# Score pairs on the same 128 rows: the key's low part in a zero-padded 128-row buffer

## The chip, the cores and the metric

The kernel runs on one core of one Trainium2 chip. The metric is the device time of one execution in microseconds (us); a time stands for a kernel as the median of its runs.

## What is computed

Causal attention with a decay between positions, then a mixture of experts with one expert per token, all in float32:

```python
B, H, S, D = 2, 8, 576, 64           # attention; 1152 tokens of 512 features
scores = (q @ k.T) / sqrt(D)         # per batch and head
cum = cumsum(log(clip(f, 1e-4, 1)))
scores = where(causal, -1e9, scores + cum[:, None] - cum[None, :])
attn = exp(scores - max(scores)); attn /= attn.sum(-1) + 1e-9
x = concat_heads(attn @ v)           # (1152, 512)
e = argmax(x @ w_gate); gate = softmax(x @ w_gate)[e]
# 8 experts, 288 slots each, first come first served; 512 -> 1024 -> 512
out[i] = gate[i] * (relu(x[i] @ w1[e]) @ w2[e])     # 0 for a token without a slot
```

## The kernel before

The work has two parts. Attention comes first: 16 heads (batch x head), two heads to a group, 8 groups. The experts follow, one after the other, with a code variant for each range of token counts.

A head's queries are cut into five tiles of 128 rows (the last has 64), the loop index `i` of `scores`. Tile `i` meets the keys up to its own end, so its score is 128, 256, 384, 512 or 576 columns wide; 576 is done as 512 and 64. Scores are computed with the fast float format `fp32r`, which rounds its operands, so queries and keys are split in a high and a low part. The tile `hi` holds, for each head, queries in its first S columns and keys in the next S. Its partitions 0 to 63 are the (rounded) values; partitions 64 to 127 hold the queries' low part and, for the keys, the same keys once more. One matmul over 128 rows (L268) thus gives the high and the low part of the query times the key. A second one (L269) adds the query's high part times the key's low part, `kl`, and uses partitions 0 to 63 alone. Both write the same PSUM bank, one of three that take turns (`spsum`).

The buffers belong to a group: `alloc` (L212 on) takes `hi`, `kl`, `raw`, `cd`, `cm` from a pool with two or three turns; `load_main` issues their loads, two on GpSimd's queue (L223, L224) and one on SyncE's (L225). `prep` makes the low parts by subtraction: `kl` at L241, the queries' at L245, mostly on GpSimd, some on VectorE; L243 makes `cm`, decay plus causal mask.

After `scores`, a tile goes through `maxima` (VectorE, L282: adds the decay and takes the row maximum), `exps` (ScalarE, L294), `transposes` (TensorE, L312, through the identity `idf`) and `evac` (copies out of PSUM, ScalarE L325 or VectorE L327). When a half of a group is complete, `av` multiplies by the values (L339, 64 columns of the array per head), `x_out` (L355) brings the result to token order and adds the gate's logits, and `x_evac` divides by the row sums. `route` (L410 to L525, on TensorE from L427) makes the tables of the experts, for the first batch half way through attention.

All engines take their instructions in the order in which the program lists them. That order is found at build time by a list scheduler in the kernel, from hand-set priorities (`BIAS`), assumed costs (S for scores, M for maxima, P for prep, and so on) and dependences; the costs do not know how many rows a matmul uses. `prologue` stands ahead of it, with 12 warm-up matmuls (L143); `filler` matmuls (L399) follow at the start.

In the experts, L847 is the first layer, L862 and L864 or L882 the second (fp32r, 128 rows throughout), L776 and L777 split the weights, L819 transposes the gathered tokens, L907 scatters the results.

Of the kernel before, what the change touches and what calls it, by code (L numbers as in the profile page):

```python
# [7 lines left out]
F32 = mybir.dt.float32  # L8
F32R = mybir.dt.float32r
# [4 lines left out]
ALU = mybir.AluOpType  # L14
# [4 lines left out]
B, H, S, D = 2, 8, 576, 64  # L19
# [5 lines left out]
P = 128  # L25
# [61 lines left out]
def attention_moe(ctx: ExitStack, tc: tile.TileContext, cap, kin, rawin, vin, f, c_iw, w1, w2,  # L87
                  c_mask, c_sel, c_idf, c_tri, c_one, c_pri, c_id, c_iota, c_slot, c_arms, out, dbg=None):
    nc = tc.nc
# [19 lines left out]
    grp = att.enter_context(tc.tile_pool(name="grp", bufs=2))  # L109
    xp = att.enter_context(tc.tile_pool(name="xp", bufs=1))  # L110
# [4 lines left out]
    def spsum(name):  # L115
        turn[0] += 1
        return banks[turn[0] % 3]
# [22 lines left out]
    def prologue():  # L140
        w = spsum("warm")
        for i in range(NWARM):
            nc.tensor.matmul(w, junk[:, :P], junk, start=True, stop=True)  # L143
        fl = pp.tile([BH, S], F32, tag="p", name="fl")
        ones = pp.tile([BH, S], F32, tag="ot", name="ones", bufs=2)
        nc.sync.dma_start(fl, f)
        nc.sync.dma_start(sel, c_sel)
        nc.sync.dma_start(mask[:, :P], c_mask)
        alloc(0)
        load_main(0, 0, 1)  # L150
        load_main(0, 1, 2)
        nc.sync.dma_start(idf, c_idf)
        load_v(0)
        nc.vector.memset(ones, 1.0)
        nc.vector.memset(rsum, 1.0)
        for t in (x_ps, t_ps[0][:, 256:], t_ps[1][:, 256:]):
            nc.vector.memset(t, 0.0)
        nc.vector.tensor_scalar(fl, fl, 1e-4, 1.0, op0=ALU.max, op1=ALU.min)
        nc.scalar.activation(fl, fl, AF.Ln)
        warm = sm.tile([P, 1], F32, tag="nb", name="warm")  # L160
        nc.scalar.activation(warm, rsum[:, 0, 0, 0:1], AF.Exp)
        nc.vector.tensor_tensor_scan(cum, ones, fl, 0.0, op0=ALU.mult, op1=ALU.subtract)
        decay_mm(0)
        for i in range(NWARM2):
            nc.tensor.matmul(w, junk[:, :P], junk, start=True, stop=True)
        nc.vector.tensor_copy(mask[:, P:2 * P], mask[:, :P])
        nc.vector.tensor_copy(mask[:, 2 * P:4 * P], mask[:, :2 * P])
        nc.vector.tensor_copy(mask[:, 4 * P:], mask[:, :S - 4 * P])
        prep(0, 0, nc.vector, 0, 256)
        prep(0, 1, nc.gpsimd, 0, 256)  # L170

    def decay_dst(a, z):
# [4 lines left out]
    def decay_mm(a):  # L177
        for z in range(3):
            t, c0, c1 = decay_dst(a, z)
            nc.tensor.matmul(t, sel[:, a], cum[:, c0:c1], start=True, stop=True)  # L180
# [27 lines left out]

    QA, KA = 0, S
    groups, vt = {}, {}  # L210

    def alloc(g):  # L212
        hi = grp.tile([P, 2, 2 * S], F32R, tag="hi", name=f"hi{g}", bufs=3)
        kl = grp.tile([D, 2, S], F32R, tag="kl", name=f"kl{g}")
        raw = grp.tile([D, 2, 2 * S], F32, tag="raw", name=f"raw{g}")
        cd = grp.tile([P, 2, S], F32, tag="cd", name=f"cd{g}", bufs=3)
        cm = grp.tile([P, 2, S], F32, tag="cm", name=f"cm{g}")
        groups[g] = (hi, kl, raw, cd, cm)

    def load_main(g, z0=0, z1=2):  # L220
        hi, kl, raw = groups[g][:3]
        hs = slice(2 * g + z0, 2 * g + z1)
        nc.gpsimd.dma_start(hi[:, z0:z1, KA:], kin[:, hs])  # L223
        nc.gpsimd.dma_start(hi[:D, z0:z1, :KA], rawin[:, hs, S:])  # L224
        nc.sync.dma_start(raw[:, z0:z1], rawin[:, hs])  # L225
# [4 lines left out]
    def load_group(g):  # L230
        alloc(g)
        load_main(g)

    def load_v(g):
        vt[g] = grp.tile([P, 2, NT, D], F32, tag="v", name=f"v{g}")
        nc.sync.dma_start(vt[g], vin[:, 2 * g:2 * g + 2])

    def prep(h, z, eng, a=0, b=S):
        hi, kl, raw, cd, cm = (x[:, h % 2] for x in groups[h // 2])
        if z == 0:  # L240
            eng.tensor_tensor(kl[:, a:b], raw[:, a:b], hi[:D, KA + a:KA + b].bitcast(F32), op=ALU.subtract)  # L241
        elif z == 2:
            eng.tensor_tensor(cm, cd, mask, op=ALU.add)  # L243
        else:
            eng.tensor_tensor(hi[D:, QA + a:QA + b], raw[:, S + a:S + b], hi[:D, QA + a:QA + b].bitcast(F32),  # L245
                              op=ALU.subtract)
# [9 lines left out]
    def scores(n):  # L256
        h, i = divmod(n, NT)
        j = h % 2
        hi, kl = groups[h // 2][:2]
        r = ROWS[i]  # L260
        q0 = i * P
        w = min(512, q0 + r)
        parts = [(0, w)] if q0 < 512 else [(0, w), (512, r)]
        st[n, "s"] = []
        qa = hi[:, j, QA + q0:QA + q0 + r]
        for c0, cw in parts:
            s = spsum(f"s{n}{c0}") if c0 == 0 else oa_ps[:, SA + D * (h % 2):]
            nc.tensor.matmul(s[:r, :cw], qa, hi[:, j, KA + c0:KA + c0 + cw], start=True, stop=False)  # L268
            nc.tensor.matmul(s[:r, :cw], qa[:D], kl[:, j, c0:c0 + cw], start=False, stop=True)  # L269
            st[n, "s"].append((s, c0, cw))  # L270

    def maxima(n):
# [326 lines left out]
    ctx.enter_context(tc.manual_schedule(engines=MAN))  # L599
    if True:  # L600
        prologue()
        ops, rel = {}, {}

# [13 lines left out]
        for g in range(NPR):  # L617
            tiles = LAST if g == NPR - 1 else TILES
            base = 2 * NT * g
            for z, u in enumerate(tiles):  # L620
                n = 2 * NT * g + u
                h, i = divmod(n, NT)
                half = 0 if i < 2 else 1
                w, r = i * P + ROWS[i], ROWS[i]
                we = (i + 1) * r

                def pr(kind):
                    return base + z + BIAS[kind][0]

                def last(k, d):  # L630
                    return [(k, *prev[-d])] if len(prev) >= d else []

                add("S", h, i, pr("S"), [(pe, 2 * max(107, min(w, 512) / 2.4) + (110 if i == 4 else 0))],
                    lambda n=n: scores(n), [("P", h, z) for z in range(3)] * (n > 1) + [("B", 0, 0)] + last("M", 3) + last("S", 1))
                add("M", h, i, pr("M"), [(dve, t_dve(w) + (77 if i else 0))], lambda n=n: maxima(n),
                    [("S", h, i), ("J", g, 0)] + last("T", 4) + last("M", 1) + [("B", h, q) for q in range(2 if i > 1 else 1)])
                add("E", h, i, pr("E"), [(act, t_act(w) + 93)], lambda n=n: exps(n), [("M", h, i), ("R", g - 2, 0)] + last("E", 1))
                add("T", h, i, pr("T"), [(pe, we / 1.2)], lambda n=n: transposes(n),
                    [("E", h, i)] + last("H", 2) + last("T", 1))
                e = HE[z]  # L640
                add("H", h, i, pr("H"), [(act, t_act(we)) if e == "a" else (dve, t_dve(we))], lambda n=n, e=e: evac(n, e),
                    [("T", h, i)] + [("A", g - 1, q) for q in range(5) if (q > 0) == half])
                prev.append((h, i))
# [22 lines left out]
            for a in range(2):  # L666
                h = 2 * g + a
                if h > 0:
                    for z in range(3 if h > 1 else 2):
                        onv = z == 1 and QE[h % 2] == "d"  # L670
                        add("P", h, z, base + BIAS["P"][3 * a + z], [(dve, t_dve(S)) if onv else (pool, 1360)],
                            lambda h=h, z=z, v=onv: prep(h, z, nc.vector if v else nc.gpsimd),
                            [("I", h // 2, 0)] + [("J", h // 2, 0)] * (z == 2) + [(k, h - 4, i) for k in "SM" for i in range(NT)])
# [51 lines left out]
        while ready:  # L725
            cand = [(max(r, free[ops[n][1][0][0]]), ops[n][0], n, ops[n][1][0][0]) for n, r in ready.items()]
            t, _, _, e0 = min(cand)
# [311 lines left out]
```

## Time and profile before

| | |
|---|---|
| runs | 381.0, 381.79, 383.2 us; median 381.79 |
| profiled execution | span 374.9 us from its first to its last instruction; its own total is not listed beside it |
| TensorE busy | matmul 311.3 us (83%), weight loads 242.0 us (65%) |
| VectorE, ScalarE, GpSimd busy | 182.3 us (49%), 153.5 us (41%), 118.5 us (32%) |
| chain that ended last | PE 60%, issue 17%, DMA 14%, DVE 4% |
| granted TensorE clock, mean | 0.915 |

In the profile PE is TensorE's matmul part, PEld its weight loads, DVE is VectorE, ACT is ScalarE, POOL is GpSimd, SP is SyncE; L12 is line 12 of the kernel. A form such as 64*128 64x512 is rows x columns of the array that a matmul uses, and then its streamed operand, partitions x columns. Busy shares are averages over two parts with different limits, so the first 150 us (attention) and the rest are to be read apart. The chain of waits goes back from the last instruction, at each step to what released it; a row's time is what the step adds to the end, which for pipelined matmuls is less than their own duration. A matmul of plain float32 stands in the trace as two records (L339, L355, L847).

### The profile page before, as it was taken

What the parts mean: (1) busy time and instruction counts of PE and PEld (TensorE: products, weight loads), DVE (VectorE), ACT (ScalarE), POOL (GpSimd) and SP (SyncE); (2) the same over time, 40 slices, a digit from 0 to 9 for tenths busy, and PEclk for the clock granted to TensorE, in tenths of its full rate; (3) what the DMA queues carried; (4) which work ended last, traced back from release to release, by engine and by line L of the source; (5) the groups of instructions that cost most, each with busy time, mean ns of one, the idle gap of its engine ahead of it and who ended that gap; (6) DMA issues with size and microseconds to landing.
All of it is one profiled execution on the core that took longest, in us unless ns stands there. A gap on an engine that the chain in (4) does not pass through costs nothing.

```text
span 374.9 us, 6090 instructions
## 1 busy us (share of the span) xinstructions
PE 311.3 (83%) x1952; PEld 242.0 (65%) x1953; DVE 182.3 (49%) x605; ACT 153.5 (41%) x416; POOL 118.5 (32%) x142
## 2 busy tenths in 40 slices
PE   7999999999999999998659558758658397877980
PEld 3555666566565656988459558757557396877980
DVE  6565667579884654673116107208053251722520
ACT  4364666666663655352044116106241433513510
POOL 4458456673547100254022203203231220300301
PEclk8599999999996999999989969969969879996997
DMA  8993996799271941438992760583917600000001
GB/s 166 252 225 101 251 370 177 138 294 366 62 200 32 388 185 31 146 93 298 410 353 99 270 237 35 203 299 116 405 43 288 243 4 11 30 8 7 34 5 47
DMA packets 19747, 64.86 MB, mean 173 GB/s; under 512 B 3503, under 2 KB 7231, under 8 KB 15074
## 3 DMA queue, kind: packets, MB, share of 16 engines
q1 hardware_dynamic: 12354, 44.86, 36.5%
q0 software_dynamic: 6224, 15.21, 14.8%
q10 hardware_dynamic: 1040, 3.44, 2.5%
q8 instruction: 36, 0.59, 0.7%
q14 instruction: 93, 0.76, 0.6%
HBM read 56.38 MB, written 9.10 MB: 175 GB/s over the span
## 4 chain that ended last, share of the span: by engine, by line
PE 60%; issue 17%; DMA 14%; DVE 4%; ACT 1%; ACTq 1%; DVEq 1%; POOL 0%; SPq 0%; POOLq 0%
DMA out<-yss,six 12%; PE bank L847 11%; PE bank L312 9%; PE bank L269 8%; PE bank L339 7%; PE bank L268 6%; PE bank L882 4%; PE bank L355 3%; PE bank L862 3%; PE bank L577 2%; PE bank L781 1%; DMA wr<-in_w 1%; DMA raw<-in_rawin 1%; PE bank L399 1%; PE bank L819 1%
## 5 line engine op out<-in xcount | busy, mean ns | idle before, releaser
L847 PE MATMUL bank<-xs,wr 128*128 128x128 f32 (+3 forms) x512 | 81.4, 326 | 49.3 <-issue 20.5
L847 PEld LDWEIGHTS bank<-xs,wr 128*128 128x128 f32 x512 | 78.4, 222 | 53.3 <-issue 32.2
L777 DVE TENSOR_TENSOR w2s<-wr,w2s 128x512 fp32r<-128x512 f32 x56 | 44.7, 816 | 74.7 <-ACT w2s L776 54.5
L776 ACT ACTIVATE w2s<-wr 128x512 fp32r<-128x512 f32 x64 | 38.9, 628 | 71.7 <-PE bank L847 40.6
L294 ACT ACTIVATE p<-p,nb 128x128 f32<-128x128 f32 (+4 forms) x80 | 47.6, 597 | 9.6 <-DVE nb L282 9.5
L907 POOL DMA_INDIRECT out<-yss,six x16 | 16.0, 1002 | 108.8 <-ACT yss L899 101.3
L325 ACT ACTIVATE p<-bank 128x256 f32<-128x256 f32 (+4 forms) x56 | 24.8, 448 | 37.3 <-PE bank L312 36.8
L282 DVE CUSTOM_DVE_ANT_0 p<-bank,cd 128x128 f32<-128x128 f32 (+2 forms) x64 | 31.1, 486 | 18.4 <-PE bank L269 10.5
L312 PE MATMUL bank<-idf,p 128*128 128x128 f32 (+2 forms) x240 | 39.2, 276 | 0.4 <-ACT p L294 0.4
L268 PE MATMUL bank<-hi 128*128 128x128 f32 (+5 forms) x96 | 38.1, 397 | 1.6 <-POOL hi L245 1.6
L269 PE MATMUL bank<-kl,hi 64*128 64x128 f32 (+5 forms) x96 | 38.0, 396 | 0.0
L862 PE MATMUL bank<-hs,w2s 128*128 128x304 f32 (+2 forms) x128 | 34.5, 352 | 0.0
L852 ACT ACTIVATE hs<-bank 128x128 fp32r<-128x128 f32 (+3 forms) x64 | 18.5, 293 | 34.6 <-PE bank L847 30.6
L807 POOL DMA_INDIRECT xg<-x_dram,gix x16 | 15.6, 977 | 53.6 <-PE bank L819 19.2
L312 PEld LDWEIGHTS bank<-idf,p 128*128 128x128 f32 (+2 forms) x240 | 23.2, 139 | 14.3 <-issue 5.9
L864 PE MATMUL bank<-hs,w2s 128*128 128x152 f32 (+2 forms) x128 | 30.6, 239 | 0.0
L339 PE MATMUL bank<-p,v 128*64 128x320 f32 (+4 forms) x224 | 30.4, 390 | 0.0
L241 POOL TENSOR_TENSOR kl<-raw,hi 64x576 fp32r<-64x576 f32 x15 | 21.5, 1437 | 15.0 <-PE bank L269 6.4
L269 PEld LDWEIGHTS bank<-kl,hi 64*128 64x128 f32 (+1 forms) x96 | 16.2, 169 | 15.5 <-issue 11.6
L853 DVE SCALAR_TENSOR_TENSOR hs<-bank,hs 128x128 fp32r<-128x128 f32 (+3 forms) x64 | 19.0, 304 | 15.0 <-ACT hs L852 14.8
L882 PE MATMUL bank<-w2s,hs 128*128 128x512 f32 x96 | 25.2, 405 | 0.0
L268 PEld LDWEIGHTS bank<-hi 128*128 128x128 f32 (+1 forms) x96 | 17.4, 181 | 11.4 <-issue 3.9
(142 smaller groups left out, 414.4 us busy)
## 6 DMA issues: line engine op xcount, KB each, us to landing
wr<-in_w SPq DMA_DIRECT2D x27, 1024.0 KB, 12.7
raw<-in_rawin SPq DMA_DIRECT2D x7, 576.0 KB, 8.1
hi<-in_kin POOLq DMA_DIRECT2D x7, 576.0 KB, 12.4
cd<-c_dram SPq DMA_DIRECT2D x7, 576.0 KB, 9.5
wr<-in_w ACTq DMA_DIRECT2D x3, 1024.0 KB, 10.9
v<-in_vin SPq DMA_DIRECT2D x8, 320.0 KB, 4.3
out<-zero SPq DMA_DIRECT2D x8, 288.0 KB, 5.4
wr<-in_w POOLq DMA_DIRECT2D x2, 1024.0 KB
```

What stands on the lines that cost most here:

```text
L268: nc.tensor.matmul(s[:r, :cw], qa, hi[:, j, KA + c0:KA + c0 + cw], start=True, stop=False)
L269: nc.tensor.matmul(s[:r, :cw], qa[:D], kl[:, j, c0:c0 + cw], start=False, stop=True)
L282: nc.vector.tensor_tensor_reduce(p[:r, a:b], s[:r, a - c0:b - c0], src[:r, a:b], -0.125, 1e30 if a == 0 else nb[:r, 0:1], ALU.add, ALU.min ...
L294: nc.scalar.activation(p[:r, :w], p[:r, :w], AF.Exp, bias=bias, scale=-1.0, accum_out=rsum[:r, h // 2 % 2, i, h % 2:h % 2 + 1])
L312: nc.tensor.transpose(t[:kw, c * r:(c + 1) * r], p[:r, c * P:c * P + kw], idf[:r, :r])
L339: nc.tensor.matmul(o[a * D:a * D + D, c0:w], vt[g][:kw, a, c], ps[a][:kw, c, c0:w], start=(c == 0), stop=(c == nk - 1), skip_group_check=True)
L776: nc.scalar.activation(w2s[:, 0, k], raw, AF.Copy)
L777: eng.tensor_tensor(w2s[:, 1, k], raw, w2s[:, 0, k].bitcast(F32), op=ALU.subtract)
L847: nc.tensor.matmul(a[:, :n], w[:, (k % 2) * FF + f * P:(k % 2) * FF + (f + 1) * P], xs[e % 2][k // 2][:, k % 2, :n], start=(k == 0), stop= ...
L862: nc.tensor.matmul(av, w2s[:, 0, k, ds], hs[:, k, :, :n], start=(k == 0), stop=(k == FC - 1), skip_group_check=True)
L864: nc.tensor.matmul(av[:, 0], w2s[:, 1, k, ds], hs[:, k, 0, :n], start=False, stop=(k == FC - 1), skip_group_check=True)
L882: nc.tensor.matmul(y_ps[0][:n], hs[:, k, y, :n], w2s[:, z, k], start=(k == 0 and z + y == 0), stop=(k == FC - 1 and z == 1))
```

## The change

`kl` becomes a buffer of 128 partitions. Its upper 64 partitions (64 to 127) are set to zero once, in the prologue, and never written again; the low part of the keys goes to partitions 0 to 63 as before. L269 (L272 in the changed kernel) then uses all 128 rows of the query tile, so that the query's low part meets zeros and the sum is the same. Both matmuls of a pair now have the same stationary operand and the same form.

For the zeros to stay, the two buffers are no longer taken from the pool by each group but made once (`kls`) and used in turn.

```diff
@@ prologue
         nc.sync.dma_start(idf, c_idf)
         load_v(0)
+        for t in kls:
+            nc.gpsimd.memset(t[D:].bitcast(F32), 0.0)
         nc.vector.memset(ones, 1.0)
...
+    kls = [xp.tile([P, 2, S], F32R, name=f"kl{z}") for z in range(2)]

     def alloc(g):
         hi = grp.tile([P, 2, 2 * S], F32R, tag="hi", name=f"hi{g}", bufs=3)
-        kl = grp.tile([D, 2, S], F32R, tag="kl", name=f"kl{g}")
+        kl = kls[g % 2]
...
@@ prep
-            eng.tensor_tensor(kl[:, a:b], raw[:, a:b], hi[:D, KA + a:KA + b].bitcast(F32), op=ALU.subtract)
+            eng.tensor_tensor(kl[:D, a:b], raw[:, a:b], hi[:D, KA + a:KA + b].bitcast(F32), op=ALU.subtract)
...
@@ scores
             nc.tensor.matmul(s[:r, :cw], qa, hi[:, j, KA + c0:KA + c0 + cw], start=True, stop=False)
-            nc.tensor.matmul(s[:r, :cw], qa[:D], kl[:, j, c0:c0 + cw], start=False, stop=True)
+            nc.tensor.matmul(s[:r, :cw], qa, kl[:, j, c0:c0 + cw], start=False, stop=True)
```

The order on TensorE, VectorE, ScalarE and SyncE stays the same, instruction by instruction. On GpSimd two memsets come in, in the prologue, behind the issues of the first loads (L223, L224; L226, L227 in the changed kernel) and ahead of the first subtraction. Before:

```order
L223 DMA hi_152<-in_kin 128x576
L224 DMA hi_152<-in_rawin 64x576
L245 ISA
L245 TENSOR_TENSOR hi_152<-raw_154,hi_152 64x256
L245 TENSOR_TENSOR hi_152<-raw_154,hi_152 64x320
```

With the change:

```order
L226 DMA hi_154<-in_kin 128x576
L227 DMA hi_154<-in_rawin 64x576
L155 MEMSET kl_114 64x1152
L155 MEMSET kl_115 64x1152
L248 ISA
L248 TENSOR_TENSOR hi_154<-raw_155,hi_154 64x256
L248 TENSOR_TENSOR hi_154<-raw_155,hi_154 64x320
```

The two memsets are new; the rest of GpSimd's list keeps its order. Waits differ on GpSimd alone: with pool buffers the first subtraction into a `kl` (of a group's first head) waited for the last L269 that read either head of the buffer's former group; now it waits for the last L269 of the head whose half it overwrites. The load of the next `hi` (L223), which stood behind that wait, now carries one of its own for the same L269.

## Rows read from the trace of the kernel before

**Rows 1.** The page's 40 equal slices of the span (9.4 us each): busy tenths of TensorE's matmuls and tenths of the granted TensorE clock.

```profile
PE   7999999999999999998659558758658397877980
...
PEclk8599999999996999999989969969969879996997
```

**Rows 2.** Busy time by stretch: the stretch and its length in us, busy us (and instructions) of each engine, granted clock, DMA share and GB/s.

```profile
core 0: us, PE busy (x) PEld busy (x) DVE busy (x) ACT busy (x) POOL busy (x), PEclk, DMA share, GB/s
...
18.00:112.50 94.50, 93.44 (x578) 56.58 (x578) 68.51 (x285) 58.12 (x171) 54.10 (x64) 1.00 0.81 219
86.00:98.30 12.30, 11.70 (x68) 7.35 (x68) 11.37 (x45) 8.32 (x24) 3.20 (x5) 1.00 0.71 230
113.30:120.10 6.80, 6.80 (x27) 3.30 (x25) 3.81 (x14) 2.23 (x6) 4.79 (x5) 0.50 0.14 39
```

**Rows 3.** TensorE's waits between 18 and 145 us, all of them: us in total, times, longest.

```profile
PE bank L427 <- DVE oh L421: 0.6, 1, 0.6
PE bank L312 <- ACT p L294: 0.4, 1, 0.4
```

**Rows 4.** The chain of waits in order of time, 61.3 to 79.1 us: start in us, what the step adds in us, engine, tile and line, and how many instructions in a row.

```profile
62.14 0.42 PE bank L268
62.56 0.43 PE bank L269
62.99 0.48 PE bank L312 x3
...
64.72 0.31 PE bank L269
65.03 0.26 PE bank L268
65.29 0.25 PE bank L269
...
68.68 0.23 PE bank L268
68.91 0.37 PE bank L269
69.27 0.17 PE bank L268
69.45 0.17 PE bank L269
69.62 0.59 PE bank L312 x4
70.21 0.23 PE bank L268
70.44 0.42 PE bank L269
70.86 0.37 PE bank L312 x2
...
72.85 0.26 PE bank L312
...
73.29 0.37 PE bank L269
...
76.59 0.06 PE bank L268
...
76.90 0.48 PE bank L312 x3
...
77.81 0.43 PE bank L268
```

**Rows 5.** The same chain in the expert layers, at 177 us (512 columns, 128 rows, weights of 128 columns) and at 202 us (L862: 304 columns, L864: 152, 128 rows).

```profile
177.54 2.09 PE bank L882 x9
...
202.25 0.18 PE bank L862
202.43 0.07 PE bank L864
```

**Rows 6.** All matmuls of the two score lines, by line: count, duration in ns (least/median/most), first and last start in us, and their forms (the four most frequent).

```profile
L268 PE MATMUL bank<-hi x96: 244/422/794, 8.4 to 143.3; 128*128 128x128 f32 x16, 128*128 128x256 f32 x16, 128*128 128x512 f32 x16, 128*64 128x512 f32 x16
...
L269 PE MATMUL bank<-kl,hi x96: 241/435/792, 8.8 to 143.6; 64*128 64x128 f32 x16, 64*128 64x256 f32 x16, 64*128 64x512 f32 x16, 64*64 64x512 f32 x16
```

**Rows 7.** GpSimd's groups by line and shape: count, busy us, mean ns of one, idle us ahead of them and what ended it.

```profile
L241 POOL TENSOR_TENSOR kl<-raw,hi 64x576 fp32r<-64x576 f32 x15 | 21.5, 1437 | 15.0 <-PE bank L269 6.4 <-DMA hi<-in_kin 5.4 <-DMA raw<-in_rawin 3.0
...
L193 POOL MEMSET zero<- 128x576 f32 x1 | 0.6, 597 | 0.0
```

**Rows 8.** GpSimd's instructions in order of time, its first subtraction: start, us, and in brackets the idle time before it and what ended it.

```profile
7.42 1.78 POOL L245 TENSOR_TENSOR hi<-raw,hi 64x256 fp32r<-64x256 f32 x2 [3.69 <-DMA raw<-in_rawin]
```

**Rows 9.** The chain of waits at the first score pair.

```profile
7.42 0.97 POOL hi L245
...
8.43 0.47 PE bank L268
```

**Rows 10.** The chain of waits behind attention, two of its gaps.

```profile
182.34 5.29 issue
...
237.60 5.24 DMA wr<-in_w
```

**Rows 11.** The chain of waits shortly ahead of the stretch at half clock.

```profile
110.82 0.93 PE bank L478 x30
```

## Prediction, made before the changed kernel ran

> **What bounds the kernel now.** I read the 40 slices first [rows 1]. PE shows a 9 in nearly every slice of the attention part (to about 150 us) and falls to 5 to 8 behind it. [...] The waits [rows 3] close the case: between 18 and 145 us PE waited for other engines twice, 1.0 us in all. In attention the path is TensorE's own queue, so time saved there is saved in the stage until another engine comes last.
>
> What is in that busy time? The chain of waits over one pair of heads [rows 4] has PE alone, so each row is what one step adds. The pattern repeats from 62.14 to 77.81 us: 15.67 us with 12 score pairs (L268, then L269). [...] The forms differ [rows 6]: L268 runs on 128 rows, L269 on 64. The neighbours agree: behind a transpose (L312, 128 rows) a 512-column L268 adds only 0.23, while the first L312 behind an L269 adds 0.26 instead of 0.11 (x2 takes 0.37, x3 0.48, x4 0.59). Each change of the row count costs 0.15 to 0.2 us.
>
> **The change, part by part.**
> *Second matmul on 128 rows.* New prices: 512 columns 0.23 (L882); 384, 256: streaming plus the 0.03 that L862/L864 shows per matmul, 0.19 and 0.14; 128: 0.12, just over the 0.11 of an L312 with a 128-column load; 64: 0.08, between 0.06 (the smallest L268 step) and 0.11.
> - L269 with 128-column weights, two of each width per period (16 of each in 8 periods, [rows 6]): 512 saves 0.195, 384 0.18, 256 0.17, 128 0.13. Twice their sum is 1.35 us.
> - The short last tile (64-column weights): 512 columns 0.37 to 0.23, and its 64-column piece 0.17 to 0.08 in L268 and in L269. Two tiles: 2 x (0.14 + 0.09 + 0.09) = 0.64 us.
> - The op behind an L269, where it too has 128 rows and 128 columns: four L312 (62.99, 70.86, 72.85, 76.90) at 0.15, an L268 at 65.03 at 0.15 and one at 62.14 at 0.19. Together 0.94 us.
> - Nothing where another change of shape remains: L339 (64 columns) behind L269, L312 behind a 64-column L269, and L268 behind 64-row transposes or 64-column L355.
>
> That is 2.93 us per period, 19% of it; 96 pairs are 8 periods, **23.4 us** of PE time. The ends: 23.4 if every row carries over; nothing if the row count is not the cause.
>
> *What of it stays on the path.* Three pairs stand before 18 us and wait for inputs: minus 0.7. From 86.0 to 98.3 us VectorE is busy 11.37 of 12.30 us [rows 2], so PE, which would need 12.3 x 0.81 = 10.0 us, gets 0.9 of its 2.3: minus 1.4. Elsewhere VectorE would rise from 0.73 to 68.51/76.8 = 0.89 of the stretch; it stands between the scores and the transposes, with ScalarE behind it, so PE will find tiles late: I take a further 3.3 us off (estimate, 15%; the ends are 0 and half the gain). Late next will be the routing of the first half, PE L427 behind VectorE L421, the one wait PE already has [rows 3], and L268 behind the row maxima of L282. Left: **18.0 us**.
>
> *Two memsets on GpSimd* ahead of its first L245. The nearest row is a memset of 128x576 in 0.597 us; by it 2 x 1152 columns take 2.4 us; by GpSimd's 64x576 subtraction, 1.437 us, they take 5.7 [rows 7]. Lower end 0. GpSimd is idle 3.69 us there, waiting for a load [rows 8], so I take 2.4 at no cost; at 5.7 the cover is gone and the first scores start 2.0 us later, since L245 is on the chain there [rows 9].
>
> *Waits.* The high-part subtraction into kl used to wait until both heads of the old buffer were read; now it waits for its own head. Behind it in GpSimd's queue are more preparations (L245, L243) and the issue of the next loads, which now carries the same wait itself. GpSimd loses 6.4 us there now [rows 7], but PE waits for none of it: no gain, and nothing newly late. Loads keep their bytes in a fifth less time: the DMA share of 0.81 [rows 2] becomes about 0.95, which can cost a microsecond or two; it is in the range.
>
> *Behind attention* nothing changes. Its long gaps, the 5.29 us of "issue" at 182.34 and the weights at 237.60 [rows 10], follow from the program's progress, so they move along; half-clock stretches that fall otherwise are worth a microsecond or two either way.
>
> Sum: the profiled span of 374.9 us becomes 356.9. The page does not list that execution's total; the runs' median is 381.79, 6.9 us above the span, and I leave those as they are: 381.8 - 18.0 = **363.8 us**.
>
> **Rivals.**
> *A: the load stays exposed.* The change lifts the wait at the switch, but the second weight load still starts only when the first matmul has streamed. Its price: at 512 columns, L269 with 128-column weights adds 0.055 us more than with 64, so a 128-column load is 0.11 and the rest of the 0.195 is 0.085. Twenty of a period's boundaries gain that: 1.7 us, 13.6 in all, 10.5 after the losses above in proportion: 371.3 us. Against it: L882 loads other weights every 0.232 us and shows no 0.11. Chance 0.08.
> [...]
>
> *B: the next engine takes over.* The round score, maxima, exponent, transpose with three score banks becomes the path in every period. For: 0.89. Against: at 0.89 VectorE still has room, and PE's waits before were 1.0 us in 127. Half the gain: 372.8 us. Chance 0.12.
>
> *C: it does not do what it says.* The switch cost hangs on something else that both forms share, and nothing moves: 381.8, or 383.8 if the memsets also outlast their cover. Chance 0.05.
>
> *D, slower: the clock.* With PE now waiting for VectorE, the granted clock falls in mid-attention, as it does at 113.3 us behind a stretch with tiny matmuls [rows 2, 11]. [...] Against: the clock stayed at 1.00 through 18 to 112.5 with the array standing at every switch, and through the wait at 98. Chance 0.04.
>
> **How the numbers follow.** Forecast 0.71, A 0.08, B 0.12, C 0.05, D 0.04. The forecast's own ends are 358 (23.4 carried over) and 370. The range takes in A and B, 357.5 to 373, and leaves out C, D and some of the tails. About 0.5%, 1.9 us, is what a measurement of this kernel can tell from none. Faster: forecast, A and B, 0.91. Same: C, 0.04. Slower: D and C's second end, 0.05.
>
> **What would show it.** Right: the 512-column pair behind a transpose adds 0.23 + 0.23 in the chain instead of 0.23 + 0.42, the next L312 0.11; the period shrinks to about 13 us; attention's last scores (L269 last starts at 143.6 us [rows 6]) start about 125 to 127; VectorE's share there is 0.85 to 0.9; PE waits a few microseconds in all for L282, L421 and the exponents. Against A: second matmuls at 0.32. For B: PE waits in every period. The memsets end before 7.4 us. Wrong: L269 still at 0.42 on 128 rows, a long stretch at half clock before 110 us, or expert layers that do not start earlier by what attention saved.

## The result, and the profile after

The changed kernel took **356.32 us** (median of 5 runs, 354.8 to 361.5) beside 381.79 us (5 runs, 375.9 to 385.1): a ratio of 0.941 [0.928, 0.955]. A second comparison, experiment 4, gave 359.0 us and 0.941 [0.934, 0.948]. On the 381.8 us of before the ratio makes 22.5 us less, 359.3 us; its interval goes from 17 to 27 us, that of experiment 4 from 20 to 25. The forecast was 18.0 less, 363.8 us, with a range from 357.5 to 373. Executions of one kernel differ by several per cent, with the clock that TensorE is granted (before, in the 17 runs that experiments 1 to 4 share: 376.35 us at a mean of 0.897, 405.77 us at 0.84), so ratios are taken between undisturbed executions, and a bare median of a few runs is not compared below.

The page of the changed kernel, its totals (busy us, share of the span, instructions), and its slices of 8.9 us (busy tenths of PE, tenths of the granted clock). In the changed kernel lines stand three further down than before: L271 and L272 are the two matmuls, L285 the maxima, L315 the transposes, L342 the sums over values, L358 the step to token order, L248 a subtraction on GpSimd.

```profile
PE 287.8 (81%) x1952; PEld 239.5 (67%) x1953; DVE 181.8 (51%) x605; ACT 153.5 (43%) x416; POOL 121.3 (34%) x144
...
PE   8999999987999999795693588567596496958980
...
PEclk9699999998999999996798799689889699996996
```

The attention part, PE full in nearly every slice, is now shorter by some 24 us, and PE still bounds it. The table by stretches says how far the others came up (columns as in [rows 2]):

```profile
18.00:95.00 77.00, 72.89 (x529) 51.12 (x529) 64.32 (x265) 54.54 (x162) 54.04 (x62) 0.98 0.99 267
95.00:130.00 35.00, 35.00 (x306) 26.47 (x303) 24.40 (x117) 23.19 (x69) 11.23 (x19) 1.00 0.59 205
```

VectorE's share is 64.32/77.00 = 0.84 (0.73 before), the DMA share 0.99 (0.81 before), and still PE is busy 72.89 of 77.00 us and all of the next 35. Its waits between 18.0 and 119.3 us, all of them, where [rows 3] had two:

```profile
PE bank L430 <- DVE oh L424: 2.0, 1, 2.0
PE bank L315 <- DVE p L330: 1.3, 1, 1.3
PE bank L315 <- ACT p L297: 0.4, 1, 0.4
PE bank L271 <- DVE nb L285: 0.2, 1, 0.2
```

Each came once, 3.9 us in all: no engine comes last in every period. The chain of waits over one period, which answers to [rows 4]:

```profile
42.51 1.81 PE bank L342 x16
44.32 0.37 PE bank L315 x2
44.69 0.23 PE bank L271
44.92 0.23 PE bank L272
45.14 0.03 PE bank L271
45.17 0.06 PE bank L272
45.23 0.49 PE bank L315 x4
45.72 0.23 PE bank L271
45.95 0.24 PE bank L272
46.19 0.22 PE bank L315 x2
...
47.67 0.18 PE bank L272
47.85 0.11 PE bank L315
...
49.19 0.45 PE bank L315 x5
49.63 0.38 PE bank L271
...
51.50 0.12 PE bank L272
...
55.15 1.81 PE bank L342 x16
```

Read it against [rows 4] row by row. A 512-column second matmul adds 0.23 or 0.24 us, the same as the first, where it added 0.42 or 0.43 with 128-column weights and 0.37 with 64. The four transposes behind a pair take 0.49 instead of 0.59, two take 0.22 instead of 0.37, and one behind 384 columns 0.11 (47.85) instead of 0.26: the 0.10 to 0.15 that the first one paid is gone. The 64-column piece (45.14, 45.17) takes 0.03 + 0.06 instead of 0.17 + 0.17, a second matmul of 384 columns 0.18 (47.67) instead of 0.37, one of 256 columns 0.12 (51.50). What stays at its old price is a first matmul behind transposes on 64 rows (0.38 at 49.63), which is still a change of rows. The period goes from 42.51 to 55.15, 12.64 us, against 15.67.

The added memsets, in GpSimd's list in order of time ([rows 8] before):

```profile
3.70 2.05 POOL L155 MEMSET kl<- 64x1152 f32 x2
7.56 1.78 POOL L248 TENSOR_TENSOR hi<-raw,hi 64x256 fp32r<-64x256 f32 x2 [1.81 <-DMA raw<-in_rawin]
```

They take 2.05 us, and GpSimd then waits 1.81 us more for the load, as it waited 3.69 before.

### The profile page after: what moved, and what is told of

It is laid out like the page before. It is cut to its first block, busy times and chain, and to the rows that moved or that the text cites. A ratio compares the mean times of both kernels' runs of the same rounds, so it can differ in the third digit from the quotient of the medians.

```text
span 356.4 us, 6092 instructions
## 1 busy us (share of the span) xinstructions
PE 287.8 (81%) x1952; PEld 239.5 (67%) x1953; DVE 181.8 (51%) x605; ACT 153.5 (43%) x416; POOL 121.3 (34%) x144
## 4 chain that ended last, share of the span: by engine, by line
PE 48%; issue 22%; DMA 15%; DVE 8%; ACT 3%; ACTq 1%; DVEq 1%; POOL 0%; SPq 0%; POOLq 0%
DMA out<-yss,six 12%; PE bank L850 11%; PE bank L315 7%; PE bank L342 7%; PE bank L271 4%; PE bank L885 4%; PE bank L272 3%; PE bank L865 3%; PE bank L358 3%; DVE w2s L780 3%; DVE p L285 2%; DMA raw<-in_rawin 1%; DMA x_dram<-xt 1%; PE bank L402 1%; PE bank L867 1%
## 5 line engine op out<-in xcount | busy, mean ns | idle before, releaser
L850 PE MATMUL bank<-xs,wr 128*128 128x128 f32 (+3 forms) x512 | 85.6, 338 | 50.8 <-issue 21.7
L850 PEld LDWEIGHTS bank<-xs,wr 128*128 128x128 f32 x512 | 82.5, 232 | 55.2 <-issue 34.3
L780 DVE TENSOR_TENSOR w2s<-wr,w2s 128x512 fp32r<-128x512 f32 x56 | 45.7, 834 | 78.7 <-ACT w2s L779 78.3
L315 PE MATMUL bank<-idf,p 128*128 128x128 f32 (+2 forms) x240 | 38.2, 271 | 1.8 <-DVE p L330 1.3
L271 PE MATMUL bank<-hi 128*128 128x128 f32 (+5 forms) x96 | 35.2, 373 | 1.2 <-POOL hi L248 0.9
L285 DVE CUSTOM_DVE_ANT_0 p<-bank,cd 128x128 f32<-128x128 f32 (+2 forms) x64 | 30.9, 483 | 6.3 <-PE bank L272 4.7
L855 ACT ACTIVATE hs<-bank 128x128 fp32r<-128x128 f32 (+3 forms) x64 | 18.5, 292 | 35.7 <-PE bank L850 33.0
L315 PEld LDWEIGHTS bank<-idf,p 128*128 128x128 f32 (+2 forms) x240 | 24.3, 140 | 12.3 <-ACT p L297 7.1
L342 PE MATMUL bank<-p,v 128*64 128x320 f32 (+4 forms) x224 | 29.5, 376 | 0.0
L272 PE MATMUL bank<-kl,hi 128*128 128x128 f32 (+5 forms) x96 | 28.8, 327 | 0.0
L867 PEld LDWEIGHTS bank<-hs,w2s 128*128 128x128 f32 x128 | 24.5, 191 | 0.0
L865 PEld LDWEIGHTS bank<-hs,w2s 128*128 128x128 f32 x128 | 24.1, 188 | 0.0
```

Of the source, the lines that this page charges most:

```text
L272: nc.tensor.matmul(s[:r, :cw], qa, kl[:, j, c0:c0 + cw], start=False, stop=True)
L285: nc.vector.tensor_tensor_reduce(p[:r, a:b], s[:r, a - c0:b - c0], src[:r, a:b], -0.125, 1e30 if a == 0 else nb[:r, 0:1], ALU.add, ALU.min ...
L315: nc.tensor.transpose(t[:kw, c * r:(c + 1) * r], p[:r, c * P:c * P + kw], idf[:r, :r])
L342: nc.tensor.matmul(o[a * D:a * D + D, c0:w], vt[g][:kw, a, c], ps[a][:kw, c, c0:w], start=(c == 0), stop=(c == nk - 1), skip_group_check=True)
L780: eng.tensor_tensor(w2s[:, 1, k], raw, w2s[:, 0, k].bitcast(F32), op=ALU.subtract)
L850: nc.tensor.matmul(a[:, :n], w[:, (k % 2) * FF + f * P:(k % 2) * FF + (f + 1) * P], xs[e % 2][k // 2][:, k % 2, :n], start=(k == 0), stop= ...
```

## The experiments

All times in these profiles are from the start of the span. The runs of before that the first four experiments share have a median of 385.45 us (17 runs), of the other four 380.35 (7 runs).

**1. The row count alone taken back.** The changed kernel, with its buffers, memsets and waits, but 64 rows in the second matmul:

```diff
-            nc.tensor.matmul(s[:r, :cw], qa, kl[:, j, c0:c0 + cw], start=False, stop=True)
+            nc.tensor.matmul(s[:r, :cw], qa[:D], kl[:D, j, c0:c0 + cw], start=False, stop=True)
```

> The changed kernel (128-row buffer, both memsets, its waits on GpSimd), but the second matmul of a pair again on the lower 64 rows of both operands. Theory 1, a change of the number of rows costs TensorE 0.15 to 0.2 us: all as in the kernel before; L272 at 512 columns adds 0.42 us to the chain, the last one starts at 143 to 144 us, the ratio to before is 0.99 to 1.01. Theory 2, a pair is cheap when both its matmuls have the same stationary operand: the same, since the operands differ again. Theory 3, the gain came from the fixed buffers and the earlier subtractions into them: as the change, last L272 at about 119 us, ratio 0.94.

Measured: 379.49 us (10 runs), a ratio to the kernel before of 1.0005 [0.995, 1.006]; the last score starts at 142.4 us (143.6 before, 119.2 with the change; 143 to 144 was expected). Its chain over a stretch that answers to [rows 4]:

```profile
60.99 0.42 PE bank L271
61.41 0.43 PE bank L272
61.84 0.48 PE bank L315 x3
...
69.06 0.23 PE bank L271
69.29 0.42 PE bank L272
```

The steps of before are back, to the hundredth. So the fixed buffers, the memsets and the looser wait of GpSimd are worth nothing that the ratio could tell (0.6%, some 2 us), and the gain hangs on the 128 rows. That GpSimd's waits were part of it is refuted.

**2. Both matmuls on 64 rows.** The kernel before with the first matmul cut to 64 rows as well; the product of the query's low part with the key is left out:

```diff
-            nc.tensor.matmul(s[:r, :cw], qa, hi[:, j, KA + c0:KA + c0 + cw], start=True, stop=False)
+            nc.tensor.matmul(s[:r, :cw], qa[:D], hi[:D, j, KA + c0:KA + c0 + cw], start=True, stop=False)
```

> The kernel before with both matmuls of a pair on 64 rows; it leaves out the product of the query's low part with the key. Theory 1: inside the pair L269 at 512 columns falls from 0.42 to 0.23 us, but the switch moves to the pair's borders: the first L268 behind a 128-row transpose rises from 0.23 to about 0.42, and L312 behind L269 stays at 0.26. About 118 switches in place of 192, so attention gains 9 to 13 us: last L269 start at 131 to 135 us, ratio 0.965 to 0.977. Theory 2, same stationary operand: the pair gains its 16 us (2.0 us per period) and nothing is paid at the border: L268 behind a transpose stays at 0.23, last L269 at about 128 us, ratio 0.958. Theory 3, fixed buffers: as before, ratio 1.00.

Measured: 373.02 us (4 runs, 363.7 to 378.9), the last score at 138.4 us, later than expected. The chain over one period:

```profile
60.25 0.59 PE bank L312 x4
60.84 0.43 PE bank L268
61.27 0.23 PE bank L269
...
64.90 0.45 PE bank L312 x5
65.35 0.23 PE bank L268
65.58 0.23 PE bank L269
...
74.66 0.43 PE bank L268
```

Within the pair the second matmul adds 0.23 us although it runs on 64 rows and reads another operand. The 0.43 has moved to the first one, behind transposes on 128 rows; behind transposes on 64 rows (64.90) the first one adds 0.23, where before it added 0.38. So neither the 64 rows in themselves nor the second operand is slow: the price is paid at each change between 64 and 128 rows, wherever it stands. The period is 13.82 us (60.84 to 74.66), 1.85 less than before: fewer changes, not none. In eight periods that is 14.8 us, more than the 9 to 13 expected. Why the last score came late stands in the table by stretches of the same run (columns as in [rows 2]):

```profile
18.00:97.00 79.00, 77.80 (x538) 49.60 (x536) 62.38 (x268) 55.35 (x164) 52.13 (x62) 1.00 0.94 254
97.70:131.80 34.10, 34.10 (x140) 20.17 (x140) 15.01 (x66) 12.98 (x37) 9.16 (x10) 0.50 0.45 167
```

For 34.1 us the granted clock was 0.50, while PE was busy all the time: 140/34.1 = 4.1 matmuls per us instead of 538/79 = 6.8. The total therefore doesn't test the sum; the steps do. The last score fits them: before, PE did 27 matmuls in the 6.80 us at half clock, 4.0 per us, against 578 in 94.50 us, 6.1, at full clock [rows 2], so each microsecond at half clock loses 0.35; 27.3 us more of it than the 6.80 of before cost 9.6, and 143.6 - 14.8 + 9.6 is 138.4 (an estimate).

**3. Fewer changes, nothing widened.** The kernel before, where a head's last tile has two pieces: first both matmuls on 128 rows, then both on 64:

```diff
             nc.tensor.matmul(s[:r, :cw], qa, hi[:, j, KA + c0:KA + c0 + cw], start=True, stop=False)
-            nc.tensor.matmul(s[:r, :cw], qa[:D], kl[:, j, c0:c0 + cw], start=False, stop=True)
             st[n, "s"].append((s, c0, cw))
+        for s, c0, cw in st[n, "s"]:
+            nc.tensor.matmul(s[:r, :cw], qa[:D], kl[:, j, c0:c0 + cw], start=False, stop=True)
```

> The kernel before with the four matmuls of each last tile (64 queries, 576 columns) in another order: both of 128 rows first, then both of 64, so two changes of rows fewer in each of 16 tiles; nothing is widened or padded. Theory 1: 32 switches at 0.10 to 0.15 us less, 3 to 5 us: last L269 at 139 to 141 us, ratio 0.987 to 0.992; L269 behind L269 adds no more than its streaming. Theory 3: no change, last L269 at 143.6 us.

Measured: 381.59 us (4 runs, 372.6 to 388.8); the last score starts at 139.6 us, 4.1 earlier than before. The chain at such a tile (in this kernel L268 is the first matmul, L271 the second, L313 the transposes), and at a tile of one piece:

```profile
67.51 0.26 PE bank L268 x2
67.77 0.41 PE bank L271 x2
...
69.00 0.43 PE bank L271
```

The four matmuls at 67.51 take 0.67 us where the order before took 0.94 (68.68 to 69.62 in [rows 4]); two changes less, 0.13 us each. Over two heads in 8 periods that is 32 changes, 4.3 us, and 4.1 came out at the last score. This is the price of a change with the operands, the rows and the bytes all as before. In the total the 4 us don't show: executions of this kernel lie 16 us apart.

**4. The change again**, unedited, beside the others.

> The changed kernel again, unedited. Theory 1 with the size of the first result: last L272 start at 119 us within 1 us, ratio 0.93 to 0.955. In the two profiles so far 24.4 us were gained at that point and 18.5 at the end, so the experts took 6 us more than in the kernel before. If that is a matter of the single execution (half-clock stretches, waits for code), the time from the first L850 to the end, 206.3 us before and 211.7 us after, comes out anywhere between 204 and 213; if it is a consequence of the change it is 210 to 213 again.

Measured: 359.0 us (6 runs), ratio 0.941 [0.934, 0.948]; last score at 118.9 us. It repeats.

**5. One change of rows less, elsewhere.** The changed kernel, with the sums over values (L342) taken over 128 rows for the last 64 keys too, where they ran on 64; rows 64 and up of that chunk of the values are zeros. The form 64\*64 64x64 becomes 128\*64 128x64; the weights' 64 columns stay:

```diff
-            kw = ROWS[c]
+            kw = P
```

> The changed kernel, with one more line on 128 rows: the product with the values (L342) takes all 128 rows for the last 64 keys too; rows 64 and up of that chunk of the values are zeros already. Theory 1: one change of rows less per group, at about 0.10 us (the step from 192 columns to the 64-row form starts 0.096 us later than streaming asks): the group of L342 that took 2.48 us takes about 2.4, the last score matmul starts 0.6 to 0.9 us earlier than 118.9 to 119.2, so at 118.0 to 118.6 us; ratio to the kernel before 0.93 to 0.95, not to be told from the change. Theory 3 (buffers): nothing, 118.9 to 119.2 us.

Measured: 356.74 us (4 runs, 351.2 to 358.5); last score at 118.7 us, against 118.9 and 119.2 in two profiles of the change (118.0 to 118.6 was expected). The chain at a group of 16 sums:

```profile
43.39 1.67 PE bank L342 x16
45.06 0.37 PE bank L315 x2
```

The group adds 1.67 us where it added 1.81 (42.51 and 55.15 in the change). By its starts each of the seven groups of 16 in this trace takes 1.67, and each of those in the three profiles of the change takes 1.81 or 1.82 at full clock. So one change less is worth 0.14 us here, a little more than the 0.10 expected. At the last score 0.2 to 0.5 us is no more than two profiles of one kernel differ by, and the total shows nothing. The two transposes behind the group still take 0.37 instead of 0.22, although both sides now use 128 rows: behind the sums something else is paid, and these runs don't show what.

**6 to 8. Where do the experts' microseconds go?** The kernel before twice more and the change once more, unedited, one run each.

> The kernel before, unedited, for one more profile. Last L269 at 143 to 144.5 us. The expert part, from the first L847 to the end, took 206.2 us in the first profile; 204.3 in the kernel with the rows back, 211.8 and 213.5 with the change. If its length is a matter of the single execution, it lies anywhere in 204 to 213 here; if attention's earlier end makes it longer, it is 203 to 207.

> As the run ahead of it, one more profile of the kernel before: execution's matter 204 to 213 us in the expert part, consequence of the change 203 to 207.

> The changed kernel, unedited, a third profile. Last L272 at 118.5 to 119.5 us. Expert part: execution's matter 204 to 213 us, consequence of the change 210 to 214.

Measured: 377.52, 400.96 and 358.13 us; last scores at 143.7, 162.3 and 121.6 us, where 143 to 144.5 was expected for the first two and 118.5 to 119.5 for the third. The second of them was at a granted clock of 0.50 from 117.9 to 155.4 us, in attention, with PE busy throughout: what rival D describes, in the kernel *before* the change. The length of the expert part (from its first L847, or the line that answers to it, to the end of the span) was

| kernel | expert part, us | the chain's row of 40 matmuls in expert 1 (the second of eight), us |
|---|---|---|
| before, its three profiles | 206.3, 206.2, 211.5 | 5.43, 7.11, 7.11 |
| without the 128 rows (experiments 1, 2, 3) | 204.4, 209.6, 210.4 | 5.43, 5.43, 7.91 |
| with the change, its three profiles | 211.7, 213.5, 209.5 | 7.09, 8.14, 7.11 |
| with the change and experiment 5's edit | 210.3 | 8.33 |

The two sets overlap, with means of 208.1 and 211.3 us. If the change made the experts longer, 203 to 207 us was expected of the kernel before and 210 to 214 of the change: 211.5 and 209.5 lie outside that, and all three new profiles lie in the 204 to 213 expected if it is a matter of the single execution. In the profile of the change most of the difference lies in experts 1 to 3 (expert 1 starts 23.8 us earlier than before, expert 4 17.7). The chain there:

```profile
158.38 5.41 issue
...
164.24 7.31 issue
...
173.38 7.09 PE bank L850 x40
```

Before, the two gaps were 5.29 and 6.69 us and the 40 matmuls 5.43; the gaps of the next expert add up to 13.67 us here and 12.70 before. The granted clock, by stretches of the same profile (columns as in [rows 2], PEclk behind the last engine):

```profile
158.00:173.00 15.00, 7.83 (x33) 6.96 (x31) 1.57 (x4) 4.06 (x9) 2.89 (x3) 0.77 1.02 364
173.40:180.50 7.10, 7.10 (x42) 7.10 (x43) 4.99 (x10) 3.32 (x8) 2.27 (x2) 0.76 0.25 95
```

Before, the stretches that answer to these two (182.0 to 196.6 and 196.6 to 202.2 us) had 0.88 and 1.00. So the 1.7 us of the 40 matmuls, and perhaps some of the gaps, are clock: PE does that group at 0.76, behind gaps of 5 and 7 us in which it had little to do. All four profiles with the change show it there (7.09 to 8.33 us), and three of the six without it (7.11, 7.11, 7.91). Whether attention's earlier end makes it likelier, or four profiles happened to fall so, these runs don't settle.

## Why the prediction was right, and where its size was off

**What bounds it: right.** PE's own queue was the path in attention (busy 93.44 of 94.50 us before, at a granted clock of 1.00 [rows 2]), and time taken out of it came out of the stage: the last score starts at 119.2 instead of 143.6 us, 24.4 earlier.

**The price of a change of rows: right**, and shown four ways: with the rows put back the old steps return (experiment 1), with both on 64 rows the step moves to the pair's border (2), with fewer changes each one less is worth 0.13 us (3), and the sums over values gain 0.14 by the same means (5). The sum by rows came to 2.93 us per period; measured 15.67 - 12.64 = 3.03, so 24.2 us in eight periods against 23.4. The excess is small steps: the 64-column piece takes 0.03 and 0.06 where 0.08 twice was taken, 256 columns 0.12 where 0.14 was; the forecast's prices for 384 and 256 columns, 0.19 and 0.14, rest on streaming times, and by them on 0.03 us more per matmul, which no row or run shows; the steps measured are 0.18 (47.67) and 0.12 (51.50). The period read also holds one wait of 0.2. A change of the weights' columns alone, from 128 to 64 at 44.69, adds nothing here: 0.23. Nor does a weight load for each matmul of L882: nine of 512 columns take 2.09 us, 0.232 each [rows 5]. The price by rows is 0.13 us in experiment 3 and 0.2 at 512 columns.

What the price is made of, the forecast left open, and the weight loads (PEld) show part of it. A pair of 512 columns before, and one with the change, from the lists in order of time (start, us):

```profile
69.96 0.48 PE L268 MATMUL bank<-hi 128*128 128x512 f32 x1
...
70.37 0.18 PEld L269 LDWEIGHTS bank<-kl,hi 64*128 64x128 f32 x1 [0.24 <-issue]
```

```profile
45.48 0.47 PE L271 MATMUL bank<-hi 128*128 128x512 f32 x1
45.56 0.19 PEld L272 LDWEIGHTS bank<-kl,hi 128*128 128x128 f32 x1
```

Before, the second matmul's load starts 0.41 us behind the start of the first, together with its own matmul (70.37); in the trace all 96 loads of L269 start 1 or 2 ns ahead of their matmul. The load engine stood idle ahead of them for 11.6 us in all, 50 times, and with the rows put back (experiment 1) ahead of those of L272 for 11.3 us, 49 times. With the change the load starts 0.08 us behind the start of the first and 0.23 ahead of its own matmul (45.79); over all 96 it is 0.17 ahead in the median. That idle time is then 0.2 us, once, and with both on 64 rows (L269 in experiment 2) 0.6 us, 3 times. So where the rows change the load is not taken ahead. That it is part of the price fits 0.195 us for 128 columns of weights and 0.14 for 64; how much of it, these runs don't separate.

**What stays on the path: mis-sized. This is the step that failed.** The prediction took 5.4 us off for pairs at the start, the VectorE-bound stretch and "a further 3.3 us". By the milestones of this profile nothing was lost: 24.2 us by the period, 24.4 at the last score (24.7 and 22.0 in the two other profiles of the change). PE's waits did grow, from 1.0 to 3.9 us, in the place that was named (L430 behind L424, 0.6 to 2.0) and at one transpose. That is 2.9 us lost. But shorter stretches at half clock gave about as much back, and the prediction had no term for these in attention (columns as in [rows 2]):

```profile
7.50:18.00 10.50, 9.57 (x38) 6.62 (x38) 8.94 (x30) 4.44 (x15) 6.33 (x8) 0.67 1.27 240
84.60:88.00 3.40, 3.40 (x21) 2.12 (x16) 1.71 (x8) 1.26 (x5) 2.87 (x8) 0.50 0.23 44
```

At the start the clock is 0.67 on average where before it was 0.51, and the stretch of 6.80 us behind 113.3 us [rows 2] is one of 3.40 here. By the price in experiment 2, 0.35 us lost per microsecond at half clock, 3.4 us less of it in mid-attention are 1.2, and up to as much at the start: most of the 2.9 that the waits cost. An estimate, since none of these runs separates the two. At the start it isn't owed to the 128 rows: experiments 1 and 2, without them, have 0.67 there as well (the three profiles of before and experiment 3 have 0.51 to 0.56), and against experiment 1's last score, 142.4, the change gains 23.2 us. In mid-attention the four traces with the 128 rows have 3.4 us at half clock or none, the six without them 6.8 to 37.5; why, these runs don't show. That VectorE at a share of 0.84 would find 15% of the gain in late tiles was too much: with three score banks a tile came late from it once for 1.3 and once for 0.2 us; the rest of the new wait is the routing's.

**The memsets: right.** 2.05 us in the place of 2.4, and hidden in the wait for the load; the first score starts at 8.57 us, against 8.43 [rows 9].

**Behind attention: partly wrong.** "They move along" holds at the start of the experts (168.6 to 144.7 us, 23.9 earlier), but the end came only 18.5 earlier. That is more than the microsecond or two allowed for half clock, and it lies in experts 1 to 3, as above; part of it is the clock there, and the rest isn't settled.

**The base: wrong, by about 5 us.** The prediction left the 6.9 us between the profiled span (374.9) and the median (381.8) as a constant. The changed kernel's profiled execution took 358.22 us for a span of 356.4, so only 1.8 us lie outside, and the profile of before was of an execution some 5 us under its median, with a granted clock of 0.90 in its experts where the five other traces without the 128 rows had 0.86 or 0.87. So the profiled span came out as forecast (356.9 against 356.4) for two misses that cancel: 6.4 us more gained by attention's last score than forecast, and 5.9 given back behind it, against an execution of before that was fast there. Against the median the gain is 22.5 us, near the full 23.4.

**The rivals.** A, that the load stays exposed, wanted 0.32 for a second matmul; it is 0.23, and its load starts 0.08 us behind the start of the first, so the load of 128 columns is hidden. A's picture of the kernel before, a second load that is not taken ahead, fits the starts of the loads above; the change lifted that too. B, the next engine in every period, is refuted by four waits in 101 us. C is refuted by experiment 1 against the change. D, the clock, did not happen in the four traces of the 128-row kernel, whose longest stretch at half clock in mid-attention is 3.4 us; what it describes happened in experiment 2 and in a run of before.

## What to carry to other kernels

Where matmuls alternate between 64 and 128 rows, compare the step that each adds to the chain with that of an equal width without a change of rows: 0.42 beside 0.23 us here (512 columns) came with the change, at which the next weight load was not taken ahead; it was paid again by whatever came next. Rows of zeros added nothing (0.23 us for the second matmul, as for the first), so widening the odd operand with a half that is zeroed once removes the change; if that can't be done, grouping what has the same rows saves some of the changes (two of four at each last tile here). When PE is the path and the next engine still has room (VectorE at 0.84 here, with three score banks), take most of the saving off, and charge first the places where a wait already stands: here the waits cost 2.9 of 24.2 us, half of it at one such place.

## What the runs showed that I had not expected

- A fully busy PE can run long at half clock: 34.1 us at a granted clock of 0.50 with PE busy 34.10 of them (experiment 2), behind a stretch at 1.00, and 37.5 us in one execution of the kernel before.
- At half clock a pair with equal rows pays nothing extra. At 87 us of the changed kernel, at a granted clock of 0.50, each of its 512-column matmuls adds 0.43 us to the chain, as six 512-column fillers (L402) did at 0.50 near the start, 2.56 us together:

```profile
86.91 0.43 PE bank L271
87.33 0.43 PE bank L272
```

- That is the very step that a second matmul showed at full clock before; from its duration alone a change of rows can't be told from a halved clock, so the granted clock of the stretch must be read beside it.
- GpSimd clears 64x1152 words in about 1.0 us (two in 2.05), less per column than its subtraction (64x576 in 1.41).
